# Attention scores as whole-row float32r products, early row sums by products, and a new table of the order

## The chip, the cores and the metric

The kernel runs on one core of one Trainium2 chip. The metric is the device time of one execution in microseconds (us); the time of a kernel is the median of several executions.

A core has TensorE (PE, matrix products), VectorE (DVE), ScalarE (ACT), GpSimd (POOL) and SyncE (SP). In this kernel SP issues all transfers. Each engine works through its own queue in order.

## The reference

The program is forgetting attention followed by two dense layers with hidden width 2048.

```python
# attention: q, k, v 4 x 8 heads x 576 x 64, f 4 x 8 x 576
scores = matmul(q, k.T) / sqrt(64)
cum    = cumsum(log(clip(f, 1e-4, 1)))
scores = where(causal, -1e9, scores + cum[:, None] - cum[None, :])
attn   = exp(scores - max(scores)); attn /= sum(attn) + 1e-9
x      = attn @ v                       # -> 2304 tokens x 512
# layer 1
h = x @ w_in;  g = max(h, 0) + alpha * min(h, 0);  x = g @ w_out
# layer 2
h = x @ w_in2; g = h * tanh(log1p(exp(min(h, 20)))); out = g @ w_out2
```

Queries and keys are about 0.6 in size, values 0.1. The weights come as float64 and are turned into float32 on the chip, from integer halves.

## The kernel before

**Number formats.** A float32 product on TensorE is issued as two instructions and goes through the array in four turns; a float32r product goes through it in one turn, with fewer bits. Where float32 precision is wanted from float32r, an operand is split into a high part (a cast) and a low part (value minus cast), and three products are added.

**Attention.** The 32 heads are worked in 16 pairs. The 576 rows are cut into row tiles of 128 (the last holds 64). In the trace a pair goes through these stages:

- *T*: ACT casts both heads' keys and queries (`kt`, `qt`, 64 rows of the contraction per head) into the float32r tiles `KM`, `QM` (four casts of 64x576).
- *M* (line 773): 12 float32r products of `QM` and `KM`, with the bias rows in the other 64 rows, give approximate scores. A VectorE reduction (line 780) after each takes the row's maximum; it writes its elements to the one scratch tile `junk`, and is followed by an instruction that reads the accumulator. Five float32 transposes (line 792) turn the maxima `M5` into a row, and ACT makes `BQ` of it (line 797).
- *S* (line 817): the scores proper, as float32 products of `kt` and `qt`. Each head has a contraction of 64, so the two heads lie in the two halves of the array's rows, side by side. A float32r product of `BK` and `BQ` adds the bias and takes the maximum off. The pieces are 288, 288, 448 + 64 and 320 + 192 columns wide, and each takes a pair of PSUM banks. ACT takes the exponential (line 827), POOL zeroes the diagonal's upper half (line 835).
- *R*: POOL adds the pieces of the exponentials into `accp` (line 853), TensorE multiplies by `ones` in float32 (line 865), 64 columns of output to each head, and ACT and DVE make the reciprocal of the sums (lines 870 to 878).
- *V* (line 899): float32 products of `vt` and the exponentials, again 64 columns of output to each head; DVE scales them (line 905) into `X`, the input of layer 1.

So three shapes of use of the array follow one another: the whole array (M, the transposes, the dense layers), halves of its rows (S), halves of its columns (R and V).

**Dense layers.** Tokens are worked in 6 blocks of 384. For blocks 0 to 2 the part of layer 1 with the first four of 16 slices of the hidden width (`group_a`, lines 943 to 945 and 1008 to 1010) runs between the products of attention as soon as the tokens are there; the rest follows after attention. Weights are loaded and converted during all stages.

**Order.** Every step is added to a `Plan` with its engine and a planned cost. `ORDER`, a list of step numbers, sets the order of what is emitted for the whole program's first part; a scheduler in `Plan` orders the rest, and the tables `PRIO` and `ENG` shift steps and pick engines. PSUM banks are taken in that order from the shares `"two"` (two pairs of banks) and `"one"` (three banks); `kt` and `qt` have three buffers each.

**Start.** 30 float32 products of `ident` (line 676) keep TensorE at work before the first product of M, and some 16 more lie between the first pair's products.

Of the kernel before, what the change touches and what calls it, by code (L numbers as in the profile page):

```python
# [22 lines left out]


ORDER = [int(x) for x in """
# [151 lines left out]


class Plan:

# [10 lines left out]
    DMA_LAG = 0.65  # L191
    PASSES = 10
    SWITCH = 0.2
    STAY = 1.5

    def __init__(self):
        self.ops = []
# [53 lines left out]
    def schedule(self, nexts, left, eng, cost, prio, lag, dma, uses=()):  # L251
# [3 lines left out]
        door = 0.0  # L255
# [943 lines left out]
```

## Time and profile before

| what | us |
|---|---|
| time before, median of 3 runs (lowest, highest) | 1011.56 (1011.18, 1013.09) |
| the profiled execution, its own time | 1013.04 |
| its span, first to last instruction | 1011.3 |
| PE busy, share of the span | 999.3, 99% |
| DVE busy | 740.1, 73% |
| ACT busy | 536.1, 53% |
| POOL busy | 341.8, 34% |

Attention lasts from the first product of M (12.0) to the last product of V (257.0); the rest of the span is the dense layers. PE is counted busy for the time that its products are in the array, which overlap, so how fast it goes is read from the starts of successive products and not from their durations. The start of a product also says when the one before it had left room.

### The profile page before, as it was taken

The page shows a single profiled execution, that of the slowest core. Times are in us where ns is not written, and L with a number is a line of the kernel's source. Part 1 is how long each engine was busy: PE and PEld are TensorE (multiplying, and loading weights), DVE is VectorE, ACT ScalarE, POOL GpSimd, SP SyncE. Part 2 cuts the span into 40 slices and gives each one's busy share as a digit, 9 for nine tenths or more (in the row PEclk, how much of TensorE's full clock was granted, in tenths as well). Part 3 has the DMA queues.
Part 4 walks back from the last instruction along what each step waited for, and adds up shares of the span by engine and source line. Part 5 has one row for each costly group of instructions (what it writes and reads, how often), then busy time and mean ns, then how long its engine had stood idle before and what let it go on. Part 6 is the DMA issues. An engine that isn't in the chain of part 4 may idle for free.

```text
span 1011.3 us, 16560 instructions
## 1 busy us (share of the span) xinstructions
PE 999.3 (99%) x5900; PEld 899.6 (89%) x5900; DVE 740.1 (73%) x1751; ACT 536.1 (53%) x1127; POOL 341.8 (34%) x351
## 2 busy tenths in 40 slices
PE   7999999999999999999999999999999999999998
PEld 6667777777999999999999999999998899989997
DVE  7787666555687765655666679877788888977975
ACT  5777676654555543233334466555454544555553
POOL 4676545545355421010101012342323322423321
PEclk9999999999999999999999999999999999999999
DMA  5344122120224323334443353000000000000000
GB/s 159 104 116 125 50 75 71 38 60 14 82 86 146 125 94 125 126 103 142 131 154 101 112 155 117 1 1 32 1 31 2 0 32 1 11 21 1 32 1 31
DMA packets 55394, 71.02 MB, mean 70 GB/s; under 512 B 6672, under 2 KB 32272, under 8 KB 55312
## 3 DMA queue, kind: packets, MB, share of 16 engines
q1 hardware_dynamic: 55312, 69.97, 21.9%
q8 instruction: 46, 0.75, 0.3%
q14 instruction: 36, 0.29, 0.1%
HBM read 56.60 MB, written 13.33 MB: 69 GB/s over the span
## 4 chain that ended last, share of the span: by engine, by line
PE 96%; DVE 3%; ACT 1%; issue 1%; DMA 0%; DVEq 0%; ACTq 0%
PE b L943 13%; PE b L945 13%; PE b L944 13%; PE b L1008 7%; PE b L1021 7%; PE b L1020 7%; PE b L1019 7%; PE b L1010 7%; PE b L1009 6%; PE b L817 6%; PE b L899 4%; PE b L773 3%; PE b L865 2%; PE b L792 1%; DVE junk L780 1%; DVE wb L558 1%
## 5 line engine op out<-in xcount | busy, mean ns | idle before, releaser
L943 PE MATMUL b<-xh,w 128*128 128x384 f32 x768 | 258.7, 337 | 0.2 <-DVE x L480 0.2
L945 PE MATMUL b<-xl,w 128*128 128x384 f32 x768 | 257.4, 335 | 0.0
L944 PE MATMUL b<-xh,w 128*128 128x384 f32 x768 | 257.2, 335 | 0.0
L1000 POOL TENSOR_TENSOR x<-x 128x384 f32<-128x384 f32 x96 | 112.3, 1171 | 250.3 <-DVE x L998 187.0
L943 PEld LDWEIGHTS b<-xh,w 128*128 128x128 f32 x768 | 144.2, 188 | 5.3 <-issue 1.0
L944 PEld LDWEIGHTS b<-xh,w 128*128 128x128 f32 x768 | 144.2, 188 | 3.1
L945 PEld LDWEIGHTS b<-xl,w 128*128 128x128 f32 x768 | 144.2, 188 | 0.0
L1008 PE MATMUL b<-g,w 128*128 128x384 f32 x384 | 130.1, 339 | 0.8 <-DVE x L971 0.7
L1010 PE MATMUL b<-g,w 128*128 128x384 f32 x384 | 128.4, 334 | 0.0
L1009 PE MATMUL b<-g,w 128*128 128x384 f32 x384 | 128.4, 334 | 0.0
L478 ACT CAST g<-x 128x384 fp32r<-128x384 f32 x120 | 61.4, 513 | 113.3 <-POOL x L1000 56.3
L1021 PE MATMUL b<-w,g 128*128 128x512 f32 x288 | 113.2, 393 | 0.0
L1020 PE MATMUL b<-w,g 128*128 128x512 f32 x288 | 113.0, 392 | 0.0
L1019 PE MATMUL b<-w,g 128*128 128x512 f32 x288 | 112.8, 392 | 0.0
L780 DVE CUSTOM_DVE_ANT_0 junk<-b,tri 128x320 f32<-128x320 f32 (+3 forms) x160 | 69.4, 434 | 45.9 <-PE b L773 36.1
L488 DVE TENSOR_TENSOR g<-x,g 128x384 fp32r<-128x384 f32 x102 | 73.3, 722 | 37.3 <-ACT g L478 36.7
L556 ACT ACTIVATE wb<-raw 128x256 f32<-128x256 f32 x128 | 52.9, 432 | 56.8 <-DMA raw<-in_moe_w_out_dram 27.6
L488 POOL TENSOR_TENSOR xl<-X,xh 128x384 fp32r<-128x384 f32 x18 | 20.8, 1161 | 168.6 <-ACT xh L478 165.8
L827 ACT ACTIVATE Pt<-b 128x288 f32<-128x288 f32 (+1 forms) x128 | 58.1, 502 | 33.4 <-PE b L817 31.4
L1008 PEld LDWEIGHTS b<-g,w 128*128 128x128 f32 x384 | 72.1, 188 | 3.6 <-DVE x L971 1.5
L558 DVE TENSOR_SCALAR wb<-wb 128x256 int32<-128x256 int32 x128 | 43.6, 356 | 42.6 <-ACT wb L556 42.2
L992 ACT ACTIVATE x<-x,two 128x384 f32<-128x384 f32 x96 | 58.6, 613 | 28.6 <-DVE x L990 28.3
(93 smaller groups left out, 1911.1 us busy)
## 6 DMA issues: line engine op xcount, KB each, us to landing
raw<-in_moe_w_in_dram SPq DMA_DIRECT2D x64, 256.0 KB
raw<-in_moe_w_out_dram SPq DMA_DIRECT2D x64, 256.0 KB
wd<-wb SPq DMA_DIRECT2D x32, 256.0 KB
raw<-wd SPq DMA_DIRECT2D x32, 256.0 KB
kt<-in_k_dram SPq DMA_DIRECT2D x16, 288.0 KB
qt<-in_q_dram SPq DMA_DIRECT2D x16, 288.0 KB
out_dram<-x SPq DMA_DIRECT2D x18, 256.0 KB
vt<-in_v_dram SPq DMA_DIRECT2D x16, 256.0 KB
```

The lines of the kernel that those rows point to most:

```text
L488: plan.add(engs, 0.0, at, lambda e: (nc.gpsimd if e == "POOL" else nc.vector).tensor_tensor(out=out(), in0=in0(), in1=in1(), op=ALU.subtra ...
L780: nc.vector.tensor_tensor_reduce(out=junk[ql, :z - a], in0=ps()[ql, :z - a], in1=tri[ql, x0 + a:x0 + z], scale=-1.0, scalar=BIG if n == 0 ...
L943: nc.tensor.matmul(ps[:, :NB], w[:, 0, c], xh[c], start=(c == 0), stop=False)
L944: nc.tensor.matmul(ps[:, :NB], w[:, 1, c], xh[c], start=False, stop=False)
L945: nc.tensor.matmul(ps[:, :NB], w[:, 0, c], xl[c], start=False, stop=(c == KC - 1))
L1000: add("POOL", c_pool(NB, 2.2), lambda e, m: nc.gpsimd.tensor_tensor(out=m, in0=e, in1=m, op=ALU.mult), [ek, mk], [mk])
L1008: nc.tensor.matmul(ps[:, :NB], w[:, 0, c], g[:, 0], start=first, stop=False)
L1009: nc.tensor.matmul(ps[:, :NB], w[:, 1, c], g[:, 0], start=False, stop=False)
L1010: nc.tensor.matmul(ps[:, :NB], w[:, 0, c], g[:, 1], start=False, stop=last)
L1019: nc.tensor.matmul(ps, g[:, 0, sl], w[:, 0], start=first, stop=False)
L1020: nc.tensor.matmul(ps, g[:, 0, sl], w[:, 1], start=False, stop=False)
L1021: nc.tensor.matmul(ps, g[:, 1, sl], w[:, 0], start=False, stop=last)
```

## The change

1. **Scores as float32r products over whole rows.** Keys and queries are split: a head's `KA`, `QA` hold the high parts in 64 rows, two bias rows at row 64 and the row of the maximum at row 96; `KB`, `QB` hold a high and a low part stacked, so that one product with a contraction of 128 gives both mixed terms. A piece of one head is the sum of a product of `KA`, `QA` and one of `KB`, `QB` (lines 804, 805 of the changed kernel), and heads follow each other. `KM`, `QM`, `BK`, `BQ` are gone: M reads the first 96 rows of `KA` and `QA`.
2. **Parts built in place.** For each pair ACT casts keys and queries into place, SP copies parts between tiles of the same memory (some six transfers of 64x576 a pair, line 735), and 64 subtractions of 64x576 give the low parts (36 on DVE, 28 on POOL). `kt` and `qt` have one buffer each instead of three; the host swaps the halves of q.
3. **Row sums of the first four pairs** (`DIRECT = 4`) are products of `ones` with all pieces of the exponentials, without `accp`. For the others the additions are shared between POOL and DVE.
4. **Maxima** are turned by float32r products of `M5` with `idr`; rows of 320 or 256 elements are then cast into `QA` on ACT (46) or DVE (18).
5. **The reduction writes in place** in PSUM; `junk` is gone.
6. **All seven banks** are one share, a bank at a time.
7. **Order.** The scheduler and its tables are removed; `ORDER`, `HOME` (engines) and `FILL` (extra warm-up products ahead of given steps) name everything. One group of 12 products of line 1008 to 1010 comes after attention instead of within it, and the start has 45 warm-up products ahead of the first product of M instead of 30. After attention the work is the same, but for 21 subtractions for the weights that go from POOL to DVE.

```diff
+HOME.update(dict.fromkeys((int(x) for x in """
...
+FILL = {63: 15, 67: 1, 75: 1, 88: 6, 85: 2, 196: 3}
...
+        for n in ORDER:
+            warm(FILL.get(n, 0))
+            self.ops[n][3]()
...
-    KEEP = 4
-    NB3 = 3
+    DIRECT = 4
...
-    plan.share("two", [(banks[2 * n], banks[2 * n + 1]) for n in range(2)])
-    plan.share("one", [banks[n] for n in (4, 5, 6)])
+    ATB = 7
+    plan.share("one", [banks[n] for n in range(ATB)])
...
+    kt, qt = (ap1.tile([P, S], F32, tag=t, name=t) for t in ("kt", "qt"))
+    KA, QA, KB, QB = heads("KA", SK), heads("QA", S), heads("KB", SK), heads("QB", S)
+    RB, RM = HALF, HALF + 32
...
+                copy(at, S, lambda T_=T_, r=r, e=e: T_[i][e][r, :S], lambda t=t, r=r: t[r], [x + "t"], [(x, i, e, w)])
...
+                        dma(at, lambda T_=T_, r=r, e=e, D_=D_, d=d: nc.sync.dma_start(D_[i][e][d, :S].bitcast(F32), T_[i][e][r, :S].bitcast(F32)),
+                            148, r=[(x, i, e, w)], w=[(x, i, e, z)], runs=1.7)
...
+                minus(at, S, lambda B_=B_, r=r, e=e: B_[i][e][r, :S], lambda t=t, r=r: t[r], lambda T_=T_, r=r, e=e: T_[i][e][r, :S].bitcast(F32),
+                      [x + "t", (x, i, e, w)], [(x, i, e, "hi" if r is hi else "lo")], "DVE")
...
-                        nc.tensor.matmul(ps()[:, :z - a], QM[i][e][:, q0:q0 + P], KM[i][e][:, a:z], start=True, stop=True)
+                        nc.tensor.matmul(ps()[:, :z - a], QA[i][e][:RM, q0:q0 + P], KA[i][e][:RM, a:z], start=True, stop=True)
...
-                                 out=junk[ql, :z - a], in0=ps()[ql, :z - a], in1=tri[ql, x0 + a:x0 + z],
+                                 out=ps()[ql, :z - a], in0=ps()[ql, :z - a], in1=tri[ql, x0 + a:x0 + z],
...
-                nc.tensor.transpose(ps()[half][:, q0 - half * W0:q0 - half * W0 + P], M5[i][:, c], ident)
+                    nc.tensor.matmul(ps()[:MC, q0 - a:q0 - a + P], M5[i][:, c], idr, start=True, stop=True)
...
+                    (nc.scalar.copy if eng == "ACT" else nc.vector.tensor_copy)(QA[i][e][RM:RM + 1, a:z], ps()[o:o + 1, :z - a])
...
-                    passes = [(kt[i3][:, ks], qt[i3][:, qs]), (BK[i][:, ks], BQ[i][:, qs])]
-                    for m, (l_, r_) in enumerate(passes):
-                        for e in range(2):
-                            nc.tensor.matmul(ps()[e][:, x:x + z - a], l_[hs[e]], r_[hs[e]], start=m == 0, stop=m == len(passes) - 1)
+                        nc.tensor.matmul(ps()[:, x:x + z - a], KA[i][e][:, ks], QA[i][e][:, a:z], start=True, stop=False)
+                        nc.tensor.matmul(ps()[:, x:x + z - a], KB[i][e][:, ks], QB[i][e][:, a:z], start=False, stop=True)
...
-        for n, j in enumerate((1, 4, 2, 3)):
+        for n, j in enumerate((1, 4, 2, 3) if pr >= DIRECT else ()):
...
+            if pr < DIRECT:
+                a0, z = x * h2, (x + 1) * h2
+                js = [(j, max(a0, j * P)) for j in range(NQ) if j * P < z]
+                            nc.tensor.matmul(ps()[hs[e], a - a0:z - a0], ones, pt_at(i, e, j, a, z), start=m == 0, stop=m == len(js) - 1)
```

On PE, between the scores of two early pairs, this stands before (a tile's number names one buffer, `b_65` to `b_72` are PSUM banks):

```order
L817 MATMUL b_67<-qt_125,kt_128 128x448
L817 MATMUL b_68<-qt_125,kt_128 128x448
L817 MATMUL b_67<-BQ_141,BK_139 128x448
L817 MATMUL b_68<-BQ_141,BK_139 128x448
L817 MATMUL b_67<-qt_125,kt_128 128x64
L817 MATMUL b_68<-qt_125,kt_128 128x64
L817 MATMUL b_67<-BQ_141,BK_139 128x64
L817 MATMUL b_68<-BQ_141,BK_139 128x64
L773 MATMUL b_71<-KM_1_135,QM_1_131 128x64
```

In the changed kernel the same place of PE, at the second pair's scores, reads:

```order
L804 MATMUL b_71<-QA_1_134,KA_1_130 128x448
L805 MATMUL b_71<-QB_1_142,KB_1_138 128x448
L804 MATMUL b_71<-QA_1_134,KA_1_130 128x64
L805 MATMUL b_71<-QB_1_142,KB_1_138 128x64
L804 MATMUL b_69<-QA_0_133,KA_0_129 128x448
L805 MATMUL b_69<-QB_0_141,KB_0_137 128x448
L804 MATMUL b_69<-QA_0_133,KA_0_129 128x64
L805 MATMUL b_69<-QB_0_141,KB_0_137 128x64
```

Scores of two heads, held in two banks at once, have become two rows for each head and bank, and no half of the array's rows is used any more.

On PE, the first pair's row sums stand before as follows (three products a head, with M's products and the first columns of V right behind):

```order
L865 MATMUL b_65<-Pt_122,ones 64x128 x2
L865 MATMUL b_65<-accp,ones 64x160 x2
L865 MATMUL b_66<-accp,ones 64x288 x2
L773 MATMUL b_71<-KM_1_135,QM_1_131 128x192
L899 MATMUL b_69<-Pt_122,vt_145 64x256 x2
L899 MATMUL b_69<-Pt_122,vt_145 64x128 x2
```

In the changed kernel PE has at that place:

```order
L863 MATMUL b_65<-Pt_123,ones 64x288 x6
L863 MATMUL b_65<-Pt_123,ones 64x192 x2
L863 MATMUL b_65<-Pt_123,ones 64x64 x2
L863 MATMUL b_68<-Pt_123,ones 64x288 x2
L863 MATMUL b_68<-Pt_123,ones 64x160 x2
L863 MATMUL b_68<-Pt_123,ones 64x32 x2
L781 MATMUL b_71<-idr,M_144 65x128 x3
L781 MATMUL b_70<-idr,M_144 65x128 x2
L896 MATMUL b_67<-Pt_123,vt_146 64x320 x6
```

The sums read the exponentials themselves, so no POOL addition stands ahead of them, and the next pair's scores, which came ahead of this place before, now come behind the first pair's V.

On DVE, the reductions of an early pair (with what each waits for on other engines or on DVE itself) stand before as:

```order
L780 ISA junk,M_142<-b_69,tri 128x448 [waits DVE_49,PE_49]
L780 ISA M_142 128x1
L780 ISA junk,M_142<-b_70,tri 128x448 [waits DVE_49,PE_49]
L780 ISA M_142 128x1
L780 ISA junk,M_142<-b_71,tri 128x320 [waits DVE_49,PE_49]
L780 ISA M_142 128x1
```

In the changed kernel DVE has, ahead of the second pair's reductions, the subtractions for its parts:

```order
L462 TENSOR_TENSOR KB_0_137<-kt,KA_0_129 64x576 [waits Activation_49]
L462 TENSOR_TENSOR QB_1_142<-qt,QA_1_134 64x576 [waits DMAHW5_49]
L462 TENSOR_TENSOR w_0_81<-wb_93,w_0_81 128x512 [waits Activation_49]
L462 TENSOR_TENSOR QB_0_141<-qt,QB_0_141 64x576 [waits DMAHW5_49,DMAHW3_49]
L768 ISA b_66,nmx<-b_66,tri 128x320 [waits PE_49]
L768 ISA nmx 128x1
L768 ISA b_67,nmx<-b_67,tri 128x320
L768 ISA nmx 128x1
```

The wait of a reduction on DVE itself has gone, and subtractions that wait for transfers stand in its queue ahead of the reductions.

## Rows read from the trace of the kernel before

**Rows 1.** Windows by stage: busy time of each engine, granted clock, DMA share, GB/s.

```profile
core 0: us, PE busy (x) PEld busy (x) DVE busy (x) ACT busy (x) POOL busy (x), PEclk, DMA share, GB/s
12.00:41.00 29.00, 26.32 (x159) 18.90 (x160) 21.80 (x84) 19.63 (x40) 13.18 (x16) 0.88 0.40 124
41.00:92.00 51.00, 50.63 (x404) 34.49 (x399) 42.06 (x148) 40.80 (x86) 35.02 (x41) 1.00 0.41 115
92.00:257.00 165.00, 164.25 (x1256) 126.16 (x1254) 97.56 (x337) 101.03 (x207) 83.87 (x106) 1.00 0.19 54
257.00:1011.30 754.30, 749.87 (x4034) 711.86 (x4032) 569.12 (x1165) 368.63 (x786) 200.44 (x165) 1.00 0.21 67
```

**Rows 2.** Timeline of PE at its start and at attention's end.

```profile
3.79 8.41 PE L676 MATMUL b<-ident 128*128 128x128 f32 x60 [3.79 <-POOL ident masks.py:199]
11.96 0.39 PE L773 MATMUL b<-KM,QM 128*128 128x320 f32 x1
...
256.99 0.44 PE L943 MATMUL b<-xh,w 128*128 128x384 f32 x1
```

**Rows 3.** Timeline of PE in one pair's scores (start, duration, line, tiles, count).

```profile
105.45 0.76 PE L817 MATMUL b<-qt,kt 64*128 64x288 f32 x4
...
106.89 0.58 PE L773 MATMUL b<-KM,QM 128*128 128x64 f32 x2
107.31 0.33 PE L943 MATMUL b<-xh,w 128*128 128x384 f32 x1
...
108.27 1.02 PE L817 MATMUL b<-qt,kt 64*128 64x448 f32 x4
...
110.86 0.36 PE L773 MATMUL b<-KM,QM 128*128 128x192 f32 x1
```

**Rows 4.** Timeline of PE: float32r products in a row, and five transposes.

```profile
104.67 0.33 PE L945 MATMUL b<-xl,w 128*128 128x384 f32 x1
104.84 0.33 PE L943 MATMUL b<-xh,w 128*128 128x384 f32 x1
...
113.85 0.71 PE L792 MATMUL b<-ident,M 128*128 128x128 f32 x5
114.31 0.42 PE L1008 MATMUL b<-g,w 128*128 128x384 f32 x1
```

**Rows 5.** Timeline of PE around one pair's row sums and products with v.

```profile
121.29 0.44 PE L865 MATMUL b<-Pt,ones 128*64 128x128 f32 x4
...
122.41 0.44 PE L1008 MATMUL b<-g,w 128*128 128x384 f32 x1
122.69 0.34 PE L1009 MATMUL b<-g,w 128*128 128x384 f32 x1
...
123.28 2.92 PE L899 MATMUL b<-Pt,vt 128*64 128x256 f32 x28
126.13 0.36 PE L773 MATMUL b<-KM,QM 128*128 128x192 f32 x1
```

**Rows 6.** Timeline of DVE in the first pair's reductions.

```profile
15.31 0.08 DVE L780 DVE_READ_ACCUMULATOR2_ANT M<- 128x1 f32 x1
15.31 0.42 DVE L560 SCALAR_TENSOR_TENSOR wb<-raw,wb 128x256 int32<-128x256 int32 x1
...
17.35 0.08 DVE L780 DVE_READ_ACCUMULATOR2_ANT M<- 128x1 f32 x1
17.57 0.62 DVE L780 CUSTOM_DVE_ANT_0 junk<-b,tri 128x448 f32<-128x448 f32 x1
```

**Rows 7.** Subtractions on DVE, 180 to 257: count, shortest, median, longest ns.

```profile
L488 DVE TENSOR_TENSOR xl<-X,xh x7: 545/547/1285, 183.6 to 242.6; 128x384 fp32r<-128x384 f32 x7
```

**Rows 8.** Waits of SP's queue over the span: us in total, times, longest us.

```profile
SPq L736 <- PE b L773: 34.0, 8, 12.4
...
SPq L736 <- DMA biasd<-Pt: 2.1, 1, 2.1
```

**Rows 9.** Casts of stage T on ACT: count, busy us, mean ns, idle ahead.

```profile
L478 ACT CAST KM<-kt 64x576 fp32r<-64x576 f32 x32 | 21.4, 667 | 2.2 <-PE b L773 1.2 <-DMA kt<-in_k_dram 0.7
```

More of the change, by code (lines that the diff above doesn't have):

```diff
@@ L25 @@
 ORDER = [int(x) for x in """
[150 rows of a table removed]
-""".split()]
-class Plan:
-    HOP = {"PE": 0.25, "ACT": 0.2, "DVE": 0.22, "POOL": 0.15, "SP": 1.0, "SWAP": 0.0}
-    OWN = {"PE": 0.0, "ACT": 0.14, "DVE": 0.12, "POOL": 0.1, "SP": 1.0, "SWAP": 0.0}
[L191 to L194, printed above, removed]
[235 rows of a table added]
+""".split()]
+HOME = {}
+HOME.update(dict.fromkeys((int(x) for x in """
[5 rows of a table added]
+""".split()), "ACT"))
+HOME.update(dict.fromkeys((int(x) for x in """
[14 rows of a table added]
+""".split()), "DVE"))
+HOME.update(dict.fromkeys((int(x) for x in """
[3 rows of a table added]
@@ L196, in __init__ @@
+""".split()), "POOL"))
+FILL = {63: 15, 67: 1, 75: 1, 88: 6, 85: 2, 196: 3}
+class Plan:
     def __init__(self):
@@ new lines, in emit @@
+    def emit(self, warm):
+        done = [False] * len(self.ops)
+        left = [len(ns) for _, ns in self.uses]
+        mine = [[] for _ in self.ops]
+        for u, (_, ns) in enumerate(self.uses):
+            for n in ns:
+                mine[n].append(u)
+        spare = {g: list(range(len(x))) for g, x in self.groups.items()}
+        for n in ORDER:
+            assert all(done[d] for d in self.ops[n][4])
+            for u in mine[n]:
+                if ("use", u) not in self.taken:
+                    self.taken["use", u] = spare[self.uses[u][0]].pop(0)
+            warm(FILL.get(n, 0))
+            self.ops[n][3]()
+            done[n] = True
+            for u in mine[n]:
@@ L394, in fox_attention__then__moe_prelu__then__moe_mish @@
+                    spare[self.uses[u][0]].append(self.taken["use", u])
+        assert all(done)
 @with_exitstack
@@ L782, in stage_M @@
                                  scale=-1.0, scalar=BIG if n == 0 else nmx[ql, e:e + 1], op0=ALU.add, op1=ALU.min,
                                  accum_out=dst() if last else nmx[ql, e:e + 1]),
-                             [bk, ("nmx", e), "tri", "zero"], ["junk", ("M5", i, c, e)] if last else ["junk", ("nmx", e)])
+                             [bk, ("nmx", e), "tri", "zero"], [("M5", i, c, e)] if last else [("nmx", e)])
         plan.stage("NM2")
-        ps, bk = plan.use("two")
-        def tr():
-            for c in range(NQ):
-                q0 = rows(c)[0]
-                half = int(q0 >= W0)
-                nc.tensor.transpose(ps()[half][:, q0 - half * W0:q0 - half * W0 + P], M5[i][:, c], ident)
@@ L793, in stage_M, with tr, fn @@
[L793 to L800 removed]
+        for half, (a, z) in enumerate(((0, W0), (W0, S))):
+            ps, bk = plan.use("one")
+            cs = [c for c in range(NQ) if (rows(c)[0] >= W0) == half]
+            def tr(ps=ps, cs=cs, a=a):
+                for c in cs:
+                    q0 = rows(c)[0]
+                    nc.tensor.matmul(ps()[:MC, q0 - a:q0 - a + P], M5[i][:, c], idr, start=True, stop=True)
+            plan.add("PE", 0.08 * len(cs), at + 6, tr, ["idr"] + [("M5", i, c, e) for c in cs for e in range(2)], [bk])
+            for e in range(2):
+                def fn(eng, e=e, ps=ps, a=a, z=z):
+                    o = e * HALF
+                    (nc.scalar.copy if eng == "ACT" else nc.vector.tensor_copy)(QA[i][e][RM:RM + 1, a:z], ps()[o:o + 1, :z - a])
+                plan.add({"ACT": c_act(z - a), "DVE": c_dve(z - a)}, 0.0, at + 6.5, fn, [bk, ("QA1", i, e)], [("QAm", i, e, half)])
@@ L821, in stage_S @@
             halves = {int(x >= W0) for _, a, z in piece for x in (a, z - 1)}
-            plan.add("PE", sum(5 * c_pe(z - a) for _, a, z in piece) + 0.01, ai, mm,
-                     [("qk", i3, j) for j in range(2)] + [("BQ", i, x) for x in halves]
-                     + [("BKr", i, e) for e in range(2)] + [("BK", i), ("kpad", i3)], [bk] + [("P", i, s, e) for e in range(2)], mode="k")
             pk = [("P", i, s, e) for e in range(2)]
             for e in range(2):
+                ps, bk = plan.use("one")
@@ new lines, in mm @@
+                def mm(ps=ps, piece=piece, e=e):
+                    x = 0
+                    for j, a, z in piece:
+                        ks = slice(j * P, (j + 1) * P)
+                        nc.tensor.matmul(ps()[:, x:x + z - a], KA[i][e][:, ks], QA[i][e][:, a:z], start=True, stop=False)
+                        nc.tensor.matmul(ps()[:, x:x + z - a], KB[i][e][:, ks], QB[i][e][:, a:z], start=False, stop=True)
+                        x += z - a
+                plan.add("PE", sum(2 * c_pe(z - a) for _, a, z in piece), ai, mm,
+                         [(t, i, e, x) for t in "qk" for x in ("A", "hi", "lo")] + [(t, i, e) for t in ("QA1", "KAb", "Kpad")]
+                         + [("QAm", i, e, x) for x in halves], [bk, pk[e]])
@@ L1125, in fox_attention__then__moe_prelu__then__moe_mish @@
     plan.add("SWAP", 0.0, T_MOE, swap1, w=["swap1"], deps=range(att_end))
-    for g_, bs in (("two", range(4)), ("one", [4, 5, 6])):
-        plan.add("SWAP", 0.0, T_MOE, lambda: None, w=[("bank", b) for b in bs], deps=[n for u in plan.uses if u[0] == g_ for n in u[1]])
+    plan.add("SWAP", 0.0, T_MOE, lambda: None, w=[("bank", b) for b in range(ATB)], deps=[n for u in plan.uses for n in u[1]])
     bA, bH = [0, 1, 2, 3], [4, 5, 6, 7]
```

296 lines of the change are left out of this document (81 added, 215 removed), and 407 rows, old and new, of tables (HOME, ORDER).

## The prediction

> **What bounds the kernel now.** I read the windows by stage first [rows 1]. From 41 us on TensorE is busy all but a few tenths of a per cent of each stage, in the dense layers too (749.87 of 754.30 us), while the next busiest engine there is DVE at about three quarters. Only in the lead, 12 to 41, does PE stand idle (2.7 us) and run at a lower granted clock, 0.88 on the mean, that is part of it at 1.2 instead of 2.4 GHz. So attention, 11.96 to 256.99 [rows 2], 245.0 us, is a queue of PE work, and a change pays what it takes off this queue, as long as no other engine becomes late. The work after attention is the same in both kernels, so I forecast a shift of attention's end. The profiled execution took 1013.04 us, 1.7 more than its span and 1.5 more than the median of the runs; the sum is made against it, and 1.5 is taken off at the end.
>
> How PE pays is in the timelines. Successive float32r products of 384 columns start 0.17 us apart [rows 4]; 384 columns at 2.4 GHz are 0.160, so a float32r product costs its columns and some 13 ns. Scores of one pair take 105.45 to 106.89 and 108.27 to 110.86, 1.44 + 2.59 = 4.03 us [rows 3]. Their 1,600 columns go through five turns (four of the float32 product for both heads together, one of the bias), 1,600 x 5 / 2400 = 3.33 us, so 0.70 are lost at the changes of shape and between. The 28 products of V take 2.85 us [rows 5] against 1,600 x 4 / 2400 = 2.67, 0.18 lost at the change. After R the first whole-array product takes 0.28 us instead of 0.17 [rows 5], and after S two products of 64 columns take 0.42 [rows 3]: 0.11 to 0.2 for a way back.
>
> **The change part by part.** All of these lie on PE's queue, where nothing hides them.
>
> *Scores.* A head takes two float32r products a piece: 4 x 1,600 / 2400 + 24 x 0.0135 = 2.99 us a pair; narrow products cost more than the rule (64 columns: 0.21 us each in [rows 3], a change of shape included), and with 0.11 for 64 and 192 columns I take 3.35, ends 2.99 and 3.45. 16 x (3.35 - 4.03) = **-10.9**, ends -16.6 and -9.3. One sentence apart from the sum: the Trainium skill, "TensorE: Matmul & The Clock Gate", Back-to-back issue gap, gives an isolated warm product N/2.4 + 2.5 ns, which would be an estimate of 2.73 us a pair and 4 us more of gain; the trace has 174 ns where that gives 162.5, so the rows decide.
>
> *Changes of shape.* The trace has 74 stretches of whole-array work, 43 of row halves and 33 of column halves between 12 and 257; in the new order I count 25, none and 25. The losses within S are in its 4.03 already. Left are 49 ways back at 0.18 (0.11 to 0.25) and 8 changes to columns at 0.18: **-10.2**, ends -6 and -14.
>
> *Turned maxima.* Five float32 transposes take 0.46 us [rows 4], 80 in all; a float32r product of 128 columns, 0.053 + 0.013, is not in the trace, its nearest row is the narrow one (0.12 without a change of shape). I take **-3**, ends -3.5 and +1.
>
> *Direct row sums.* They have the columns and the shape of V, 2.85 us instead of 1.12 (121.29 to 122.41) [rows 5], four times: **+7.0**. What they spare is POOL's work, which no PE time rests on except in the lead.
>
> *Start.* 15 more warm-up products ahead of M: 60 instructions took 8.2 us [rows 2], so 30 take up to 4.1. M may have to wait for its bias rows in part of that time anyway, and 13 warm-ups instead of 16 lie between the first pair's products. **+1.3**, ends -1 and +3.5.
>
> *Lead.* 29 us from 12 to 41 hold 2.7 us without work and, at 0.88 of the clock, 3.5 us of slowness [rows 1]. Before, the first pair's sums stand behind the second pair's scores and POOL's additions; after, ahead of both. And a reduction no longer waits for the one before: behind a reading of the accumulator the next reduction starts 0.22 us after it (17.35, 17.57), while another instruction starts at once (15.31 twice) [rows 6]. I take half of the 6.2 us: **-3**, ends -6 and +2 (the second pair's scores come later, so its exponentials may become late).
>
> *Waits that are new.* DVE gets 36 subtractions of some 0.55 to 0.8 us (547 ns median for 384 columns [rows 7], 576 here), row casts and a third of the additions, and loses the 0.22 us waits of most of its 192 reductions: by my count 14 us of work more, some 24 of waiting less, on an engine that is busy 161 of 245 us [rows 1]. In the lead it is fuller (21.8 of 29) and weights are converted there. SP gets six transfers a pair, each of which waits for its cast; behind it in SP's queue stand the loads of keys, bias and v, and for those stage T and M of the next pair. ACT's casts stay some five a pair at 0.67 us [rows 9]. Cover is good where dense work lies between (from 92 on), thin in the first four pairs. I take **+2.5**, ends 0 and +12.
>
> The group of 12 products that moves behind attention makes attention 2.1 us shorter (12 x 0.174) and the rest as much longer: nothing. The 21 subtractions that move to DVE after attention lie beside a PE that is never short of work: nothing; if that cover were gone for a few of them, at 0.55 to 0.8 us each, 0 to +2 together.
>
> Sum: -10.9 - 10.2 - 3 + 7.0 + 1.3 - 3 + 2.5 = **-16.3**; 1013.0 - 16.3 = 996.7, less 1.5: **995 us**. Attention then ends near 238.6, and the last 2.1 us of its work come after.
>
> **The rivals.**
>
> *PE keeps the whole gain.* If the waits are nil and the lead gives 6: -16.3 - 2.5 - 3 = -21.8, and with S at 2.99 some 5 more: 984 to 990. For it: PE has waited for next to nothing since 41 us in a kernel whose buffers were as tight. Against: each pair now needs more steps of DVE, SP and ACT in less time.
>
> *DVE and POOL in each other's way.* The subtractions are of two tiles in SBUF. Seven such on DVE took 547 ns in the median, but the longest 1285, 0.74 more [rows 7], with POOL at work beside it. Should 64 subtractions meet such a delay in one case of three, DVE and POOL are late by 21 x 0.74 = 15.5 us, and in the early pairs half of it would reach PE: +8, with a ring that is a little tight +5 to +13, 1000 to 1008. The Trainium skill, "SBUF — State Buffer", SBUF: two separate sides, has a rule for it: an instruction of DVE with two inputs in SBUF and one of GpSimd that reads SBUF share a pair of ports, and the second waits until the first has ended. By that rule every meeting would cost, and the row with 547 in the median and 1285 at most agrees that some do and most do not.
>
> *Slower than before: the ring of one buffer.* `kt` and `qt` are now filled only when the pair before has read them for the last time (a subtraction on DVE or POOL), and the transfers between tiles stand in SP's one queue. The chain from one pair's scores to those that use the same tiles two pairs later is four casts (2.7), a transfer (2.1, the round trip through memory in [rows 8]), twelve reductions of some 0.55 (6.5), the turn and the row casts (1.5) and the scores (3.4): 16 us for two pairs, where the forecast has 2 x 14.2 us (attention from 11 to 239 for 16 pairs). A head of line that waits costs up to 12.4 us in SP's queue now [rows 8]. If that befalls each pair once, the chain is 16 + 24.8 = 41 us, 20 a pair; it decides from a period of 15.3 us, that is a stall of 7.4 us a pair. Just above, at 8 us a pair (period 16), attention would end near 268: 1024. Against it: SP waits that long 8 times only, and PE never waited for it.
>
> *The change does not do what it says.* If the float32r scores were paced by loading their weights, as narrow products are now, S would stay near 4 us a pair and the gain fall by 10.9: 1006. Against: M's products of the same widths and shape are paced by their columns.
>
> **How the numbers follow.** The forecast (990 to 1000) gets 0.50, the whole gain 0.17, DVE and POOL in each other's way 0.18, no cheaper scores or some of both (1006 to 1013) 0.07, slower by the ring 0.08. Below 984 and above 1006 lie together about 0.2, so the **range is 984 to 1006**. A measurement of this kernel can tell some 0.2%, 2 us, from no change: faster than 1009.5 gets 0.88 (0.50 + 0.17 + 0.18 and half of the 0.07), the same 0.04, slower 0.08.
>
> **What would show it.** In the new trace the scores of a pair should take 3.0 to 3.45 us of PE and stand within whole-array work without a change of shape around them; a direct row sum 2.85; the first product after attention start near 239 instead of 257; PE idle between 41 and there stay below 4 us. Reductions should follow the reading of the accumulator without the 0.22 us. The forecast is wrong if PE waits in the early pairs for DVE's subtractions, for the maxima or for SP's transfers, with gaps of some us in every pair, if subtractions take well over 0.8 us on DVE, or if products after the scores start late in spite of the single shape.

## The result

| kernel | us, median (lowest to highest) | ratio to before, 95% interval |
|---|---|---|
| before | 1012.33 (1011.18 to 1017.25) | |
| changed | 1025.35 (1024.03 to 1025.94) | 1.0124, 1.0098 to 1.0150 |

The change made the kernel 13 us slower, where 16 us of gain were forecast. The profiled execution of the changed kernel took 1024.99 us, its span 1023.2.

The stages of the changed kernel answer to [rows 1]; the fifth line is the stretch behind attention from 320 to 480 us, the sixth the one after it.

```profile
core 0: us, PE busy (x) PEld busy (x) DVE busy (x) ACT busy (x) POOL busy (x), PEclk, DMA share, GB/s
12.00:41.00 29.00, 27.35 (x198) 22.52 (x197) 24.97 (x85) 17.42 (x36) 10.60 (x20) 0.95 0.72 194
41.00:92.00 51.00, 47.66 (x365) 38.66 (x365) 46.04 (x152) 42.37 (x90) 28.07 (x35) 0.96 0.59 166
92.00:257.00 165.00, 156.89 (x1175) 133.53 (x1175) 144.15 (x416) 111.08 (x233) 93.27 (x110) 1.00 0.43 116
320.00:480.00 160.00, 153.03 (x862) 148.41 (x860) 135.01 (x328) 69.41 (x165) 25.25 (x20) 1.00 0.57 182
480.00:560.00 80.00, 80.00 (x463) 80.00 (x463) 25.32 (x43) 21.81 (x44) 3.68 (x4) 1.00 0.02 7
```

In attention PE no longer has work at all times: 3.3 us without any from 41 to 92 and 8.1 from there to 257, where it was 0.4 and 0.8. DVE is busy 144 of 165 us instead of 98. PE's longest waits in attention are for DVE's casts of maxima (first line) and for a dense step of DVE (second):

```profile
PE b L804 <- DVE QA L786: 2.3, 3, 1.1
PE b L940 <- DVE x L965: 2.1, 1, 2.1
```

And a stretch that the forecast had called unchanged has 7 us of idle PE of its own; the same two windows of the kernel before read:

```profile
320.00:480.00 160.00, 160.00 (x925) 160.00 (x924) 105.60 (x259) 66.55 (x156) 28.36 (x21) 1.00 0.37 119
480.00:560.00 80.00, 80.00 (x464) 80.00 (x463) 50.47 (x124) 29.48 (x73) 7.95 (x6) 1.00 0.41 132
```

There PE is full and DVE's work is spread evenly, 106 and then 50 us; in the changed kernel it is 135 and then 25, and DMA's share is 0.57 and then 0.02. The waits of PE from 320 to 480 in the changed kernel (us in total, times, longest) name DVE's steps between the two products of layer 1:

```profile
PE b L1007 <- DVE g L462: 2.9, 4, 1.4
PE b L940 <- DVE X L965: 2.4, 2, 1.4
PE b L940 <- DVE X L968: 1.3, 2, 0.6
```

To see where the time goes, take the start of the n-th product of the dense layers, which are the same 4,320 in both kernels. The 289th, near attention's end, starts at 254.8 instead of 257.0: attention gains **2.1 us** between these two profiles. (In e3 below, which has the attention of the kernel before, the 289th starts at 255.3, so the gain is small in any case.) The 801st starts 0.5 us earlier, the 1,001st 3.7 later, the 1,601st 10.6 later, and the last 11.4 later. So the loss has two places: attention, where 14 of the forecast's 16 us are missing, and the stretch from 347 to 497 us (the 801st to the 1,601st product), which costs **11** of the 13.5 us lost behind attention.

What PE's own work costs came out much as forecast. The first lines are PE's timeline in the lead, the later ones in a late pair (start, duration, line, tiles, count):

```profile
3.37 12.19 PE L652 MATMUL b<-ident 128*128 128x128 f32 x90 [3.37 <-POOL ident masks.py:199]
15.32 2.12 PE L763 MATMUL b<-KA,QA 96*128 96x320 f32 x10
...
28.48 2.96 PE L863 MATMUL b<-Pt,ones 128*64 128x288 f32 x32
31.37 0.51 PE L781 MATMUL b<-idr,M 128*65 128x128 f32 x5
31.81 2.93 PE L896 MATMUL b<-Pt,vt 128*64 128x320 f32 x28
...
239.59 0.39 PE L804 MATMUL b<-QA,KA 128*128 128x448 f32 x1
...
240.17 0.38 PE L804 MATMUL b<-QA,KA 128*128 128x288 f32 x1
...
240.52 0.30 PE L804 MATMUL b<-QA,KA 128*128 128x320 f32 x1
...
241.01 0.39 PE L804 MATMUL b<-QA,KA 128*128 128x448 f32 x1
```

448 + 64 columns of a head take 0.58 us (239.59 to 240.17), 288 take 0.35 behind them, 320 + 192 take 0.49; with the second 288 at 0.27 (238.09 to 238.36 in the same pair) a head is some 1.69 and a pair 3.4 us, against 4.03 in [rows 3]. A direct row sum takes 2.89 (28.48 to 31.37).

### The profile page after: what moved, and what is told of

It reads as the page before. It is cut to its first block, busy times and chain, and to the rows that moved or that the text cites. A ratio compares the mean times of both kernels' runs of the same rounds, so it can differ in the third digit from the quotient of the medians.

```text
span 1023.2 us, 16641 instructions
## 1 busy us (share of the span) xinstructions
PE 994.3 (97%) x5812; PEld 912.6 (89%) x5812; DVE 801.7 (78%) x1824; ACT 552.2 (54%) x1154; POOL 319.9 (31%) x337
## 4 chain that ended last, share of the span: by engine, by line
PE 67%; DVE 14%; DMA 9%; ACT 4%; issue 3%; POOL 1%; SPq 0%; DVEq 0%; ACTq 0%; POOLq 0%
PE b L940 10%; PE b L941 10%; PE b L942 10%; PE b L1018 7%; PE b L1016 7%; PE b L1017 6%; PE b L1005 3%; PE b L1007 3%; PE b L1006 3%; DMA raw<-in_moe_w_out_dram 3%; DMA raw<-in_moe_w_in_dram 3%; DVE wb L536 3%; DVE wb L538 2%; PE b L896 2%; PE b L804 2%
## 5 line engine op out<-in xcount | busy, mean ns | idle before, releaser
L462 DVE TENSOR_TENSOR g<-x,g 128x384 fp32r<-128x384 f32 x110 | 76.0, 695 | 34.2 <-ACT g L452 31.7
L965 DVE SCALAR_TENSOR_TENSOR X<-X,alph,b 128x384 f32<-128x384 f32 x65 | 39.6, 611 | 61.5 <-ACT X L959 61.5
L991 DVE SCALAR_TENSOR_TENSOR b<-x 128x384 f32<-128x384 f32 x96 | 61.0, 635 | 27.7 <-ACT x L990 27.0
L1007 PEld LDWEIGHTS b<-g,w 128*128 128x128 f32 x384 | 72.1, 188 | 6.2 <-DVE g L462 6.2
L462 POOL TENSOR_TENSOR xl<-X,xh 128x384 fp32r<-128x384 f32 x24 | 27.0, 1132 | 160.3 <-ACT xh L452 143.1
L1005 PEld LDWEIGHTS b<-g,w 128*128 128x128 f32 x384 | 72.1, 188 | 3.7 <-DVE x L965 2.3
```

The lines of the kernel that those rows point to most:

```text
L462: plan.add(engs, 0.0, at, lambda e: (nc.gpsimd if e == "POOL" else nc.vector).tensor_tensor(out=out(), in0=in0(), in1=in1(), op=ALU.subtra ...
L1005: nc.tensor.matmul(ps[:, :NB], w[:, 0, c], g[:, 0], start=first, stop=False)
L1007: nc.tensor.matmul(ps[:, :NB], w[:, 0, c], g[:, 1], start=False, stop=last)
```

## The experiments

Each kernel was run beside the kernel before; ratios are to it. "Old order behind" names the first experiment, on which most others build.

### The order behind attention

The changed kernel's attention, with the order and engines of the kernel before behind attention's last product (numbers from there on, e1):

```diff
 ORDER = [int(x) for x in """
 ...
-1699 1712 1714 1710 1523 1700 1701 1702 1703 1520 1522 1524 1705 1900 1907 1902 1901 1915 1916 1917 1918 1920
+1699 1712 1714 1710 1523 1700 1701 1702 1703 1520 1522 1524 1704 1740 1741 1742 1743 1706 1705 1841 1780 1719
 ...
```

> The changed kernel's attention, and behind attention's last product the order and the engines of the kernel before. Theory (the loss has two places): the changed order converts the weights of layer 2 beside fewer products behind attention, DVE cannot follow, and that alone costs 12 us between 320 and 470 us; so this runs at 1013 us, with PE idle below 5 us behind attention. Rival (the loss behind attention is something that attention leaves over, work in arrears on DVE or another state of the memory): 1022 to 1026.

Measured: **1012.73** (1.0007, 0.9988 to 1.0026). PE from 320 to 480 is full again, and the last product of the dense layers starts 0.7 us before that of the kernel before:

```profile
320.00:480.00 160.00, 160.00 (x925) 160.00 (x925) 105.58 (x255) 66.00 (x156) 25.26 (x20) 1.00 0.38 120
```

The counterpart, the kernel before with the new order behind its own attention (e3):

```diff
-        for _ in range(self.PASSES):
...
+        self.taken = {("use", u): b for u, b in enumerate(TAKEN)}
+        order = [n for n in EARLIER if n not in tail]
...
+        for n in LATER:
+            put(n)
```

> The kernel before up to attention's last product, and behind it the order and engines of the changed kernel. Theory (the order behind attention costs 12 us by itself): 1023 to 1025 us. Rival (only together with the new attention): 1011 to 1013.

Measured: **1026.88** (1.0140, 1.0123 to 1.0158). The order behind attention costs 12.6 us under one attention and 15 under the other, so it needs nothing from the new attention. What of it is DVE's work, the changed kernel tells without DVE's three conversion steps for the weights of layer 2 (e11):

```diff
-        plan.add("DVE", c_dve(HM, True), at, lambda: V.tensor_scalar(
+        plan.add("DVE", c_dve(HM, True), at, lambda: None if left else V.tensor_scalar(
             wb(), wb(), 3, None, op0=ALU.logical_shift_left), [wbk], [wbk], port=BOTH)
...
```

> The changed kernel with its own order behind attention (1025.4 us), but of the conversion of layer 2's weights DVE's three steps a half are left out; loads, ACT's step, stores and fetches stay. If DVE's amount of work in that stretch makes the loss behind attention: 10 to 12 us faster, 1013 to 1015. If the order of transfers or ACT's queue does: 1020 or more.

Measured: **1016.01** (1.0039, 1.0022 to 1.0056), 9.3 us faster, with the window

```profile
320.00:480.00 160.00, 159.87 (x920) 158.93 (x919) 72.14 (x141) 70.80 (x170) 21.16 (x20) 1.00 0.58 187
```

The loads, stores and DMA share stay as in the changed kernel, and PE is full: some nine of the twelve or thirteen us hang on DVE's conversions, which are crowded into fewer products. The order itself shows the crowding: 64 conversions stand beside the 252nd to 496th group of three products, where they stood beside the 269th to 699th.

But DVE isn't busy throughout that stretch. It is idle 25 of the 160 us in the changed kernel, and for 15.2 of them it stands at the head of its queue for ACT's first conversion step, which itself waits for transfers of weights:

```profile
DVE wb L534 <- ACT wb L532: 15.2, 23, 2.7
ACT wb L532 <- DMA wd<-wb: 29.2, 18, 4.0
```

The chain that ended last from 345 to 480 us lies to 45% in such transfers and to 21% in DVE's three steps, and from 320 to 480 SP's loads of weights wait 73 us for the last of these steps to free their buffers. So load, ACT's step, DVE's steps and the next load form a ring, and e11 takes DVE's links out of it together with DVE's work. It doesn't tell whether the amount of work or the ring makes the nine us.

Two attempts to move only the weights' steps failed (e2 puts the old places into the new order, e8 the new places into the old order):

```diff
-1699 1712 1714 1710 1523 1700 1701 1702 1703 1520 1522 1524 1704 1740 1741 1742 1743 1706 1705 1841 1780 1719
...
```

> The changed kernel, where behind attention only the steps that load, convert, store and fetch weights are put at the products beside which they stand in the kernel before; all other work keeps the new order and engines. If the place of the weights' conversion alone is the cause behind attention: 1013 to 1015 us. If the order of the rest or the engines count: 1018 to 1025.

> As the run with the old order behind attention (1012.7 us), but the steps that load, convert, store and fetch weights stand at the products beside which the new order has them (layer 2's conversions on the mean 117 products earlier, 64 of them beside 244 groups of products instead of 430). If these steps' place alone makes the loss behind attention: 1021 to 1026 us. If the order or engines of the other work do: 1012 to 1015.

Measured: 1112.86 and 1100.04. I had placed these steps by the product that they stand beside and ahead of the other engines' steps there, so that the queues of ACT and DVE stand still behind steps that wait for transfers (in e2 ACT waits 49 us between 260 and 600 for loads of the output weights alone). They say nothing on the question.

### DVE in attention

The old order behind, with the subtractions left out from the third pair on (e4), or only those of DVE (e6), or only those of POOL (e7):

```diff
-                minus(at, S, lambda B_=B_, r=r, e=e: B_[i][e][r, :S],
+                (minus if pr < 2 else skip)(at, S, lambda B_=B_, r=r, e=e: B_[i][e][r, :S],
...
-                        nc.tensor.matmul(ps()[:, x:x + z - a], KA[i][e][:, ks], QA[i][e][:, a:z], start=True, stop=False)
-                        nc.tensor.matmul(ps()[:, x:x + z - a], KB[i][e][:, ks], QB[i][e][:, a:z], start=False, stop=True)
+                        nc.tensor.matmul(ps()[:, x:x + z - a], KB[i][e][:, ks], QB[i][e][:, a:z], start=True, stop=True)
+                        nc.tensor.matmul(ps()[:, x:x + z - a], KA[i][e][:, ks], QA[i][e][:, a:z], start=True, stop=True)
```

> As the run with the old order behind attention, but from the third pair on the 56 subtractions of the low parts are left out, and of a piece's two products the second overwrites the first (so the low parts do not count in the result; TensorE does the same work). Theory (DVE, and POOL beside it, cannot follow in attention): PE's 13 us of gaps in attention shrink to 4 or so, and this runs 8 to 10 us faster than that one, about 1004 us. Rival (casts, transfers between tiles and the one buffer of keys and queries set the pace): at most 3 us faster, 1010 or more.

> As the run without subtractions (1001.5 us), but only DVE's 31 subtractions from the third pair on are left out; POOL makes its 25. If DVE's amount of work is the bound (31 x some 0.98 us = 30 us taken from DVE): 8 to 10 us faster than with all of them, 1003 to 1005. If it is the meeting of DVE and POOL at their shared memory port: 5 to 6 us, 1007, and as much from leaving out POOL's.

> The counterpart: only POOL's 25 subtractions from the third pair on are left out; DVE makes its 31. If DVE's amount of work is the bound: 0 to 3 us faster than with all of them, 1010 to 1013, with the mean of a DVE subtraction falling from 0.98 towards 0.75 us. If the meeting at the port is: 5 to 6 us faster, 1007.

Measured: **1001.50** (0.9893), **1001.25** (0.9897, 0.9869 to 0.9925) and **1007.50** (0.9948). Leaving out DVE's 31 gives all that leaving out all 56 gives. The windows 41 to 92 and 92 to 250 of e1, then of e6:

```profile
41.00:92.00 51.00, 46.49 (x366) 37.36 (x367) 46.87 (x154) 41.51 (x89) 27.11 (x34) 1.00 0.63 172
92.00:250.00 158.00, 151.01 (x1122) 127.58 (x1121) 137.08 (x397) 106.94 (x225) 92.10 (x108) 0.98 0.44 116
```

```profile
41.00:92.00 51.00, 48.19 (x383) 38.59 (x384) 41.59 (x153) 43.14 (x92) 26.89 (x36) 1.00 0.69 187
92.00:250.00 158.00, 155.03 (x1165) 133.24 (x1162) 120.64 (x376) 108.31 (x229) 90.37 (x109) 1.00 0.43 114
```

With 22 us of DVE gone, PE has 6 us of work more in the same time and 60 more products. PE doesn't wait for the parts themselves: its listed waits in e1 from 41 on are mostly for steps that stand in DVE's queue with the subtractions, foremost

```profile
PE b L803 <- DVE QA L785: 2.3, 3, 1.2
PE b L762 <- DVE M L767: 2.1, 3, 0.9
```

What POOL's subtractions cost (5.2 us) is not the same again: taken beside DVE's, they give nothing. e7 came out at the 1007 that was expected if the two engines' meeting makes the loss, and not at the 1010 or more for DVE's amount of work; but DVE's subtractions fell only from 0.98 to 0.90 us in the mean, 2.8 us in all. One way in which they reach DVE stands in the changed kernel's timelines, first DVE, then PE, then POOL:

```profile
97.12 2.64 DVE L462 TENSOR_TENSOR QB<-qt,QA 64x576 fp32r<-64x576 f32 x1
...
100.37 0.60 DVE L965 SCALAR_TENSOR_TENSOR x<-x,alph,b 128x384 f32<-128x384 f32 x1
```

```profile
101.02 0.45 PE L940 MATMUL b<-xh,w 128*128 128x384 f32 x1 [2.13 <-DVE x L965]
```

```profile
96.02 3.13 POOL L836 TENSOR_TENSOR accp<-Pt 128x896 f32<-128x896 f32 x1 [1.22 <-PE b L853]
```

A subtraction that takes 0.75 us in the median began at 97.12 while POOL added two tiles, and ended 0.61 us after POOL did, at 99.76; four steps later PE had waited 2.1 us. The Trainium skill, "SBUF — State Buffer", SBUF: two separate sides, says that such a pair of instructions does not share its ports but that the second stands until the first has ended, and here that agrees. Of DVE's 36 subtractions in the changed kernel the nine that took over 0.9 us all began while a POOL instruction was running and ended some 0.6 us after it; the other 27 took 0.74 to 0.76 us. It is not the main term: DVE's subtractions come to 0.99 us in the mean, 0.23 above the median, 8.3 us in all 36.

The counterpart adds waits of DVE on itself without touching the chain of parts: old order behind, with the scratch tile back (e9).

```diff
-                                 out=ps()[ql, :z - a], in0=ps()[ql, :z - a], in1=tri[ql, x0 + a:x0 + z],
+                                 out=junk[ql, :z - a], in0=ps()[ql, :z - a], in1=tri[ql, x0 + a:x0 + z],
```

> As the run with the old order behind attention (1012.7 us), but the reductions write their elements to the one scratch tile again instead of back to PSUM. Theory (DVE's time is the bound in attention, and a reduction behind a reduction costs 0.22 us more with the scratch tile, less some 0.05 us that the reading of the accumulator takes longer in place: 0.17 x some 180 = 30 us of DVE): 8 to 12 us slower, 1021 to 1025. Rival (the wait in the scratch tile cost nothing that counts): 1011 to 1014.

Measured: **1025.96** (1.0136, 1.0110 to 1.0163), 13.2 us slower. Attention's time follows DVE's queue in both directions. That DVE's amount of work alone sets it is not shown: four runs below take work off DVE and are not faster.

The rival of the forecast that had foreseen the time was the ring through the one buffer of keys and queries. With two buffers (e5):

```diff
-    kt, qt = (ap1.tile([P, S], F32, tag=t, name=t) for t in ("kt", "qt"))
+    kt, qt = ([ap1.tile([P, S], F32, tag=t + str(i), name=t + str(i)) for i in range(2)] for t in ("kt", "qt"))
...
```

> As the run with the old order behind attention (1012.7 us), but keys and queries have two buffers each, so that a pair's load does not wait for the last reading of the pair before. If the ring through the one buffer sets the pace in attention: 4 to 8 us faster, 1005 to 1009. If DVE's load of work, or DVE and POOL in each other's way, does: at most 2 us off, 1011 to 1014.

Measured: **1011.76** (0.9994, 0.9978 to 1.0011). In e1 the loads of keys and queries did wait in SP's queue until subtractions had freed the one buffer, 57 us in attention, most of it for DVE:

```profile
SPq L696 <- DVE QB L461: 26.8, 8, 7.3
```

With two buffers these waits are gone and the time stays. The buffer is not the cause.

### The price of the direct sums and of the start

```diff
-                js = [(j, max(a0, j * P)) for j in range(NQ) if j * P < z]
+                js = [(0, a0)]
...
```

(The small number added to the sums is raised to 1 as well; it changes no time that is argued with here.)

> As the run with the old order behind attention (1012.7 us), but the direct row sums of the first four pairs take the first piece of the exponentials alone (the others are left out of the sum), 576 columns instead of 1,600: 1.75 us of TensorE less in each of the four. If TensorE sets the pace in the first pairs, as the sum supposed: 6 to 7 us faster, 1006. If DVE does: 0 to 3 us, 1010 to 1013.

Measured: **1015.52** (1.0041, 1.0023 to 1.0059): 7 us of PE's work less, and no gain, rather 2.8 us lost. PE's window there, against 1.00 in e1:

```profile
41.00:92.00 51.00, 42.93 (x283) 33.50 (x282) 46.23 (x151) 41.60 (x89) 27.57 (x34) 0.93 0.62 167
```

DVE is as busy as in e1 (46.2 of 51), and the time that PE saved became idle. The granted clock fell to 0.93 in that window, part of it at 1.2 GHz. The trace shows what came ahead of the fall: a wait of PE for DVE's cast of a maximum, then a stretch at half speed.

```profile
76.57 0.44 PE L803 MATMUL b<-QA,KA 128*128 128x448 f32 x1 [2.56 <-DVE QA L785]
```

```profile
77.50:84.30 6.80, 6.80 (x27) 6.32 (x26) 5.07 (x21) 3.96 (x9) 4.42 (x6) 0.50 0.45 141
```

All three falls of the clock in attention come during or right behind PE's three longest gaps (2.1 to 2.6 us). In attention e10's profile has 17 us at 1.2 GHz, e1's 6.8 and e6's none; at half speed the difference between the first two is some 5 us of PE's work. The mean granted clock also goes with the time of single executions: e1 took 1009.8 us at 1.000 and 1018.0 at 0.992, e10 1013.2 at 0.995 and 1021.2 at 0.987. So a gap on PE can be paid a second time by the clock. That this is the whole of the 2.8 us is likely, but not tested.

Without the 15 added warm-up products (v6; the entry 63 of `FILL` left out):

```diff
-FILL = {63: 15, 67: 1, 75: 1, 88: 6, 85: 2, 196: 3}
+FILL = {67: 1, 75: 1, 88: 6, 85: 2, 196: 3}
```

> As the run with the old order behind attention (1012.7 us), but without the 15 warm-up products that were added ahead of M (30 as in the kernel before). If they delay the first product of M (15.3 us instead of 12.0) and the delay reaches attention's end: 1009.5 to 1011. If M waits for its operands until then, or the time is lost again beside a full DVE, or the clock falls: 1012 to 1015.

Measured: 1011.77 (0.9996, 0.9986 to 1.0006), 1 us under e1 with intervals that overlap. The later start does not reach the end.

### Can the work be moved?

Four tables of engines on top of the old order behind: additions for the sums to POOL and casts of maxima to ACT (v1), the additions alone (v3), all 36 of DVE's subtractions to POOL (v2), only those of keys (v4). Their edits are entries of `HOME`, as in v3:

```diff
-102 156 172 483 564 567 597 685 770 831 858 917 948 949 1008 1035 1036 1095 1096 1122 1124 1180 1184 1210 1268
...
+102 156 172 483 564 567 831 917 1008 1095 1096 1180 1184 1268 1269 1357 1359 1360 1445 1446 1526 1528 1556
...
```

> As the run with the old order behind attention (1012.7 us), but DVE's 19 additions for the row sums go to POOL and its 18 casts of row maxima to ACT: 23 us less on DVE in attention, some 27 more on POOL, 7 more on ACT. If DVE's amount of work is the bound (0.37 us of time for each us of work, by the run without DVE's subtractions: 11.5 for 31): 6 to 9 us faster, 1004 to 1007, faster than both kernels. If POOL's longer chain from exponentials to sums comes in its place: 1011 or more.

> As the run with the old order behind attention (1012.7 us), but only the 19 additions go to POOL; the casts of the maxima stay as they are. With the run that moved both at 1020.2: if ACT's queue ahead of the casts made that loss, this is at 1006 to 1010 (15 us less on DVE at 0.37); if POOL's chain from exponentials to sums did, at 1016 or more.

> As the run with the old order behind attention (1012.7 us), but all 36 of DVE's subtractions go to POOL (64 there). If DVE's amount of work is what counts: 11.5 us gained from DVE, less 36 x 0.2 = 7 that POOL's subtractions cost by the run without them: 1007 to 1009, faster than both kernels. If POOL's longer time for each (1.42 us against 0.75) makes the pairs' scores late: 1012 or more.

> As the run with the old order behind attention (1012.7 us), but the 17 subtractions of keys on DVE go to POOL, those of queries stay. Between the two: if DVE's amount counts, 1009 to 1011; if POOL's slowness does, 1012 to 1015.

Measured: 1020.20 (1.0080), 1014.33 (1.0033), 1024.92 (1.0125) and 1016.89 (1.0042). Each takes work off DVE and none is faster. v3 lies between its two expected ranges and v4 above both. In v1 PE waits for ACT's casts, in v2 for POOL's additions and its zeroing of exponentials, which now stand behind subtractions of 1.4 us (PE's waits in v1, then in v2):

```profile
PE b L807 <- ACT QA L789: 5.3, 5, 2.6
```

```profile
PE b L854 <- POOL accp L837: 3.5, 3, 2.0
PE b L864 <- POOL Pt L819: 3.1, 1, 3.1
```

So amount and place both count: with DVE, ACT and POOL this full, a step moved within a fixed order becomes late somewhere else. The clock has a part in these times too: its median over the executions is 0.9925 in v1 and v4, 0.990 in v2 and 0.996 in v3, against 0.997 in e1. How much, no run here separates.

### Versions that beat both

One part alone, on the kernel before: the reductions write back to PSUM (e12).

```diff
-                                 out=junk[ql, :z - a], in0=ps()[ql, :z - a], in1=tri[ql, x0 + a:x0 + z],
+                                 out=ps()[ql, :z - a], in0=ps()[ql, :z - a], in1=tri[ql, x0 + a:x0 + z],
```

> The kernel before with one part of the change alone: the reductions write back to PSUM instead of to the scratch tile. DVE waits behind itself some 150 times less, 0.17 us each, 25 us of DVE in attention. If that counts only where DVE is the bound, it gives nothing here, PE being busy 157 of 158 us from 92 on: 1010 to 1012.5. If it counts by itself: 1000 to 1005.

Measured: **1009.01** (0.9969, 0.9959 to 0.9979), 2.9 us under the kernel before and 16 under the changed one. I had expected nothing. In its profile the first dense product starts at 52.9 us, against 54.5 in e3, which has the same attention with the scratch tile: over half of the gain is in the lead, where PE's idle time from 12 to 41 is 1.9 us, against 2.6 in e3.

What bounds attention once the added work is gone (v7):

```diff
-                        nc.tensor.matmul(ps()[:, x:x + z - a], KA[i][e][:, ks], QA[i][e][:, a:z], start=True, stop=False)
-                        nc.tensor.matmul(ps()[:, x:x + z - a], KB[i][e][:, ks], QB[i][e][:, a:z], start=False, stop=True)
+                        nc.tensor.matmul(ps()[:, x:x + z - a], KA[i][e][:, ks], QA[i][e][:, a:z], start=True, stop=True)
...
```

> As the run with the old order behind attention (1012.7 us), without any low parts: no subtractions, no product of KB and QB, and only the 32 transfers that the high parts need; the scores then have float32r's precision. Without subtractions it was 1001.5; the product left out is 1.65 us of PE a pair, 26 in all. If PE is the bound once DVE is relieved: 977 to 985. If DVE's rest or ACT takes over at once: 990 to 1000.

Measured: **994.57** (0.9833, 0.9819 to 0.9848). Of 26 us of PE's work taken away beside e6, only 6.7 came out. PE is then idle 9 of the 209 us from 41 to 250, so something else paces it again. Part of it is the clock: v7's profile has 17 us at 1.2 GHz in attention and e6's none, which is an estimated 8.5 us of the 20 that are missing. Which engine makes the gaps, no run here tells.

## Why the prediction was wrong

- **PE is the bound now: right** for the kernel before. The error was to carry it over to a kernel in which PE has less and DVE more to do, and to price DVE's part as a small sum at the end.
- **Scores (-10.9): right.** A pair takes some 3.4 us instead of 4.03 (forecast 3.35).
- **Changes of shape (-10.2), direct sums (+7.0): right as PE's work** where rows show it. From 12 to 257 the changed kernel has 26 stretches of whole-array work, none of row halves and 25 of column halves, and the sums take 2.89 us (forecast 2.85). What a way back is worth was not measured apart. The sums' 7 us were not on the path: e10 took them out and gained nothing. While DVE sets the pace, such terms can't be added up.
- **Turned maxima (-3): too large by its own row**, which gives 16 x (0.46 - 0.33) = 2.1 us. Five take 0.30 to 0.35 us where nothing disturbs them, against 0.46 before.
- **Start (+1.3): undersized**, M begins 3.4 us later (15.32 against 11.96), and it did not matter (v6). **Lead (-3): not seen apart.** The first dense product starts 2.0 us earlier, at 54.3.
- **New waits (+2.5, at most 12): the step that failed in attention.** DVE's subtractions alone cost 11.5 us (e6). The forecast counted 14 us of DVE work more, which its own prices do not give: 36 subtractions at 0.55 to 0.8 us are 20 to 29 us, before the casts and additions that it named beside them. Measured from 12 to 257, the subtractions make some 34 us, the 18 casts 8 and the 19 additions 15. One term was missing: the reading of an accumulator takes 0.13 instead of 0.08 us, 10 us over 192. A subtraction takes 0.75 us undisturbed, within the price, but 0.99 in the mean. DVE's busy time from 12 to 257 rose from 161 to 215 us, by 54. At 144 of 165 us it is no longer something that hides work. Without DVE's subtractions attention gains 12.8 us, most of the forecast's sum.
- **The clock behind the lead: no term.** The forecast counted a lowered clock in the lead alone. With PE's new gaps it falls later too: e1's profile has 6.8 us at 1.2 GHz between 92 and 257, which costs some 3.4 us, and e6's none. So part of what e6 gains is the clock.
- **"The work after attention is the same: nothing": the other step that failed.** The work is the same, its order is not. The change had a new table for the whole program, and I read only its part in attention. Behind attention it costs 12.6 us (e1). Some 9 of them need DVE's conversions, which stand beside fewer products, in a ring with the loads of weights (e11).
- **The rivals.** "Slower by the ring" gave 1024, near the measured time, by a mechanism that e5 refutes and with attention ending near 268, where its last product starts at 252.5 and the order behind it costs the rest. That its time came near is chance. "DVE and POOL in each other's way" exists (97.12 above) but is the smaller part of DVE's excess, 8.3 of 54 us. Its reading of [rows 7] was wrong: of the seven subtractions only the long one (191.28) met a POOL instruction, so they show no meeting without cost. The right mechanism, a DVE too full to hide its work, stood in the text only as a cover that was "thin in the first four pairs".

What stays open: which steps of the order behind attention make the last 3 of its 12.6 us, since e2 and e8 did not isolate them; whether DVE's work or the ring of loads and conversions makes the other nine; how much of attention's loss is the clock; and how the gain of 5.2 us without POOL's subtractions splits between the port and the chain.

## What to carry to other kernels

When a change takes work off the bound and puts work on the next engine, add up that engine's new busy time by stage from durations, its slowed ones too, and compare it with the *shortened* stage: here 215 us, where the forecast left a stage of some 227. When a change brings a new table of the order, compare where every engine's work stands beside the bound in the whole program, not only where the edit is meant: counting conversions per hundred products would have shown the crowding. And try the cheap part of a large change by itself: one operand, written back in place, beat the whole.

## What the runs showed of the hardware

- A reduction with an accumulator that writes back to PSUM in place is followed by a reading of the accumulator of 134 ns in the median instead of 82, but the next reduction starts behind it without the 0.22 us of [rows 6]. The changed kernel's rows (count, shortest, median, longest ns, then two in order of time):

```profile
L768 DVE DVE_READ_ACCUMULATOR2_ANT M<- x160: 74/134/146, 16.9 to 232.4; 128x1 fp32r x128, 64x1 fp32r x32
```

```profile
83.87 0.14 DVE L768 DVE_READ_ACCUMULATOR2_ANT M<- 128x1 fp32r x1
83.87 0.26 DVE L768 CUSTOM_DVE_ANT_0 b<-b,tri 64x64 f32<-64x64 f32 x1
```

- A subtraction of two tiles on DVE that begins while POOL works ends some 0.6 us after POOL's instruction (nine of 36 in the changed kernel, 0.92 to 2.64 us long); the others take 0.74 to 0.76 us, those too during which a POOL instruction begins.
- Taking work from an engine that isn't the bound can fail to save time: with 7 us less of PE's work in the first pairs the gaps grew, e10's profile has 17 us at 1.2 GHz in attention where e1's has 6.8, and the kernel became 2.8 us slower.
- A kernel with gaps on PE scatters with the clock: ten executions of e1 lie between 1009.8 us (mean granted clock 1.000) and 1018.0 (0.992), nine of e12, all at 0.999 to 1.000, between 1008.3 and 1009.6.
